# Eighteen pieces of the first five expert tiles multiplied unsplit, conversion's additions on GpSimd too, six products of the identity first

## The chip, the cores and the metric

The program runs on one core of one Trainium2 chip. The metric is the device time of one execution in microseconds; lower is better. [...]

## What is computed

Three layers in float32, one after the other: block-causal attention, an expert layer in which every token goes to one expert, and a dense gated layer.

```python
# attention: q, k, v are (4, 8, 576, 64); position i sees j where i // 64 >= j // 64
scores = np.where(mask, q @ k.T / 8, -1e9)
attn = softmax(scores) @ v
x = attn.transpose(0, 2, 1, 3).reshape(2304, 512)
# experts: expert_emb (8, 512), w1 (8, 512, 1024), w2 (8, 1024, 512), tau 0.1
xn = x / (norm(x) + 1e-6);  en = expert_emb / (norm(expert_emb) + 1e-6)
logits = xn @ en.T / tau
expert_idx = argmax(logits, axis=1);  gate_w = softmax(logits)[expert_idx]
out[mask] = gate_w[mask, None] * (relu(x[mask] @ w1[e]) @ w2[e])   # for each expert e
# dense layer: w_in (512, 2048), w_out (2048, 512)
h = out @ w_in
result = (h / (1 + exp(-h))) @ w_out
```

## The kernel before

**A planner sets every order.** Nothing is issued where it is written. `_Plan` records each operation with the engines that may run it (`either`, `copy`, `tt`, `relu` give two alternatives, `sub` only VectorE), its estimated cost (`_cost`) and what it depends on. `issue` then plays a list schedule: at each step it takes, on the engine that is free first, the ready item with the lowest due time, chooses the engine of items that may go to two, and writes the instructions out in that order. `STAY_NS` is what an item on TensorE is set back by if it needs the array in another shape than the item before (64 rows for scores, 64 columns for the attention's output, the full 128 by 128 for the rest); `CHANGE` is the time that the plan gives such a switch. `_best` builds the program, takes due times from the finished plan backwards (`latest`), builds again, three times in all, and keeps the plan that is shortest by its own estimate. So one changed number can change the order on every engine.

**Precision.** A float32 product is done in one of two ways. Split: both operands are written as a rounded high part and a low rest (`split` for weights: a cast on ScalarE or VectorE and a subtraction on VectorE), and `three` issues three fast products (type fp32r). Unsplit: one product of plain float32, which TensorE runs as two instructions, here without any work on other engines.

**Attention** (`_attention`) handles 16 pairs of heads, staged so that scores of one pair (`s`), transposes of the probabilities of another (`pt`), products with v (`o`) and rows of the output (`e`) of others lie side by side. Softmax takes row maxima on VectorE (`mx`), the exponential on ScalarE (`p`). The norm of the expert embedding is made once, early (`experts`): a square root and a dummy exponential on ScalarE, each of which makes ScalarE load another table of functions.

**Conversion.** `_Convert.piece` rounds the dense layer's weights from raw bits in 32 pieces (16 of `win`, 16 of `wout`), spread over attention and experts. The last step of a piece is an integer addition: on GpSimd for pieces 0 to 11, on VectorE from piece 12 on.

**Experts** (`_layers`). Tokens are sorted into tiles of 128 with one expert each; `_Route` finds the places. For a tile `s`, `xt` transposes the gathered rows (`xg`, two buffers), `first` multiplies with four pieces of w1 (in the order 2, 3, 1, 0), `ht` transposes the hidden rows, `second` multiplies with four pieces of w2. All eight pieces lie in `wraw`, one buffer, refilled for the next tile two pieces at a time if the expert changes. `DIRECT` says how many pieces of each weight of a tile are multiplied unsplit: `(2, 1, 1, 1)`, so pieces 0 and 1 of tile 0 and piece 0 of tiles 1 to 3, for w1 and for w2: ten. Where there are any, `whole` keeps a plain copy of the transposed rows. In PSUM, `xt` and the rest of the tile use the three banks of tag `t`; the banks `a` are for the dense layer's sums. From tile 2 on, chunks of the dense layer (`chunk`: `up` makes `g`, `down` makes `o`) are merged with the tiles.

**The end.** After a chunk's last `down`, `store` copies each of three blocks of the result to SBUF and sends it with an indirect transfer from GpSimd's queue. Just ahead of the transfer, GpSimd copies the column of row numbers (`ix`).

## Time and profile before

| | us |
|---|---|
| median of three runs | 892.42 (892.38 to 893.39) |
| the profiled execution | 892.14 |
| its span, first to last instruction | 890.4 |
| TensorE busy | 856.0 (96%) |
| VectorE busy | 722.6 (81%) |
| ScalarE busy | 554.1 (62%) |
| GpSimd busy | 121.9 (14%) |

The profile is one execution recorded by the hardware; its own time stands 1.7 us above its span. Times in its rows are microseconds from the span's start unless marked ns. PE is TensorE, PEld its weight loads, DVE VectorE, ACT ScalarE, POOL GpSimd, SP SyncE; a q behind the name is the engine's queue. The arrow in `h<-w1s,xt` points from what is read to what is written. The attention fills about the first 210 us; the tiles of the experts run from there to about 610 us, with the dense layer merged in from about 275 us; after that the dense layer is alone. Almost every operation is recorded by one helper line of the planner (L199, or L258 for grouped products), so rows are told apart by the names of the tiles.

### The profile page before, as it was taken

Reading aid. Unit: us, or ns where it says so; the run is one execution under the profiler, and the core shown is the slowest. Engines: PE = TensorE matmul, PEld = TensorE weight load, DVE = VectorE, ACT = ScalarE, POOL = GpSimd, SP = SyncE. Lnnn points to the kernel's source line nnn. Section 1 sums busy time; section 2 is a strip of 40 time slices with the busy share of each in tenths; the row PEclk is TensorE's granted clock in tenths of the full one; section 3 lists DMA queues with packets and bytes.
Section 4 is the critical chain, followed back from the end, with each engine's and each line's share of the span. In section 5 each row is a group of like instructions: output and inputs, shape, how many; then the busy total and the mean of one; then the engine's idle time right before and its main releaser. Section 6 shows DMA issues by size and latency. Waiting matters only on the chain.

```text
span 890.4 us, 13848 instructions
## 1 busy us (share of the span) xinstructions
PE 856.0 (96%) x4986; PEld 713.9 (80%) x4986; DVE 722.6 (81%) x1264; ACT 554.1 (62%) x1128; POOL 121.9 (14%) x162
## 2 busy tenths in 40 slices
PE   5999999999999999999999999999999999999995
PEld 4777677766567888888888888888999999999994
DVE  6989798988999799999888888887677767667672
ACT  7889787976467588888866665665334235334332
POOL 3013131123310000211311111002001001001001
PEclk9999999999999999999999999999999999999998
DMA  6545362473044477530102230342002002000000
GB/s 191 164 122 165 111 180 82 122 256 82 13 159 140 140 272 272 178 94 26 71 24 76 68 119 24 107 132 72 34 1 71 1 1 72 1 0 36 1 1 35
DMA packets 38440, 82.75 MB, mean 93 GB/s; under 512 B 5208, under 2 KB 13400, under 8 KB 38368
## 3 DMA queue, kind: packets, MB, share of 16 engines
q1 hardware_dynamic: 32736, 63.47, 22.2%
q0 software_dynamic: 5632, 18.36, 6.7%
q8 instruction: 40, 0.66, 0.3%
q14 instruction: 32, 0.26, 0.1%
HBM read 123.23 MB, written 13.11 MB: 153 GB/s over the span
## 4 chain that ended last, share of the span: by engine, by line
PE 65%; POOL 0%; POOLq 0%; issue 0%; ACT 0%
PE o L199 22%; PE g L199 22%; PE y L199 9%; PE h L199 9%; PE ht L199 2%; PE xt L199 1%; PE yt L199 1%; POOL out_dram L1559 0%; POOLq L1838 0%; ACT os L199 0%; POOL ix L1558 0%; POOLq L1559 0%
## 5 line engine op out<-in xcount | busy, mean ns | idle before, releaser
L199 PE MATMUL o<-w,g 128*128 128x512 f32 x864 | 234.2, 396 | 0.0
L199 PE MATMUL g<-yt,w 128*128 128x384 f32 x1152 | 230.7, 337 | 0.0
L199 PEld LDWEIGHTS g<-yt,w 128*128 128x128 f32 x1152 | 203.9, 188 | 13.8
L199 PEld LDWEIGHTS o<-w,g 128*128 128x128 f32 x864 | 160.0, 188 | 27.4 <-ACT g L199 0.3
L199 ACT ACTIVATE sg<-g 128x384 f32<-128x384 f32 x96 | 47.4, 494 | 141.9 <-PE g L199 141.8
L199 PE MATMUL y<-w2s,ht 128*128 128x512 f32 x450 | 131.3, 402 | 1.2 <-DVE w2s L199 1.2
L199 PE MATMUL h<-w1s,xt 128*128 128x512 f32 x450 | 110.4, 394 | 3.4 <-DVE xt L199 2.0
L199 PEld LDWEIGHTS h<-w1s,xt 128*128 128x128 f32 x450 | 83.5, 188 | 22.1 <-ACT h L199 2.0
L199 DVE TENSOR_TENSOR w1s<-wraw,w1s 128x1024 fp32r<-128x1024 f32 x75 | 91.2, 1221 | 11.4 <-ACT w1s L199 11.1
L199 DVE TENSOR_TENSOR w2s<-wraw,w2s 128x1024 fp32r<-128x1024 f32 x75 | 91.0, 1224 | 10.0 <-ACT w2s L199 8.7
L199 PEld LDWEIGHTS y<-w2s,ht 128*128 128x128 f32 x450 | 81.2, 188 | 16.3 <-DVE w2s L199 2.7
L199 ACT ACTIVATE p<-s,mx 128x576 f32<-128x576 f32 (+4 forms) x160 | 82.7, 527 | 15.7 <-DVE mx L199 12.9
L199 DVE TENSOR_TENSOR w<-win,w 128x512 fp32r<-128x512 f32 x96 | 66.0, 689 | 24.0 <-ACT w L199 23.4
L199 ACT CAST w2s<-wraw 128x1024 fp32r<-128x1024 f32 x68 | 71.0, 1051 | 14.2 <-PE h L199 7.4
L199 ACT CAST g<-sg 128x384 fp32r<-128x384 f32 x96 | 49.4, 514 | 39.9 <-DVE sg L199 38.3
L258 PE MATMUL s<-ks,qs 64*128 64x288 f32 (+4 forms) x576 | 61.3, 344 | 13.1 <-ACT p L199 7.7
L199 DVE TENSOR_REDUCE mx<-s 128x1 f32<-128x576 f32 (+3 forms) x96 | 64.6, 705 | 10.5 <-PE s L258 9.5
L199 ACT CAST w1s<-wraw 128x1024 fp32r<-128x1024 f32 x53 | 55.6, 1054 | 20.7 <-PE y L199 15.2
L199 DVE TENSOR_TENSOR w<-wout,w 128x512 fp32r<-128x512 f32 x96 | 65.6, 683 | 0.2 <-ACT w L199 0.2
L199 ACT CAST w<-win 128x512 fp32r<-128x512 f32 x75 | 46.6, 625 | 28.7 <-PE o L199 28.6
L258 PEld LDWEIGHTS s<-ks,qs 64*128 64x128 f32 x576 | 46.5, 199 | 20.0 <-ACT p L199 10.5
L199 DVE TENSOR_TENSOR sg<-g,sg 128x384 f32<-128x384 f32 x96 | 53.3, 556 | 10.6 <-ACT sg L199 7.9
(194 smaller groups left out, 1127.5 us busy)
## 6 DMA issues: line engine op xcount, KB each, us to landing
wraw<-in_moe_w_dram SPq DMA_DIRECT2D x76, 1024.0 KB
wbits<-in_moe_w_in_dram SPq DMA_DIRECT2D x16, 512.0 KB
wbits<-in_moe_w_out_dram SPq DMA_DIRECT2D x16, 512.0 KB
k<-in_k_dram SPq DMA_DIRECT2D x16, 288.0 KB
q<-in_q_dram SPq DMA_DIRECT2D x16, 288.0 KB
v<-in_v_dram SPq DMA_DIRECT2D x16, 256.0 KB
x_rows<-xe POOLq DMA_DIRECT2D x16, 256.0 KB, 4.1
wraw<-in_moe_w_dram SPq DMA_DIRECT2D x8, 512.0 KB
```

The costliest lines, as they stand in the source:

```text
L199: alts = {e: (lambda eng, m=m, a=a, k=k: getattr(eng, m)(*a, **k), self._cost(e, m, a, k), self._shares(e, m, a, k) if e != "tensor" else ...
L258: eng.matmul(out, a, b, **kw)
```

## The change

- `DIRECT` becomes `(2, 2, 2, 2, 1)`: eighteen unsplit pieces instead of ten, over five tiles.
- The conversion's addition from piece 12 on may go to VectorE or GpSimd, as the planner finds. So may small additions and products of the routing (`tt`, `ts` of `_Route`).
- Six products of the identity with itself into an unused PSUM tile (`t_warm`) stand first on TensorE. A dummy exponential stands first on ScalarE, and the root of the embedding's norm is made on VectorE by three rounds of a Newton step (`_root`) instead of ScalarE's table.
- `xt` of tiles 2 to 4 uses a bank of tag `a` instead of `t` (`XC = 5`).
- The copies of the row numbers are made when a chunk's first `down` begins; behind each store, GpSimd makes a copy of `ix` to a spare tile.
- The planner: `STAY_NS` 500 and 1500 (two sets of three builds) instead of 2000, `CHANGE` 95 instead of 190, and other costs for some products, reciprocals and subtractions. A term for work that is bound to one engine and still to come (`coming`) has weight 0. Paths under `OM`, `PF`, `CA`, `CB`, `GROOT` are written but not taken.

```diff
-DIRECT = (2, 1, 1, 1)
+DIRECT = (2, 2, 2, 2, 1)
-STAY, STAY_NS, CHANGE = 30, 2000.0, 190.0
+STAY, STAY_NS, CHANGE = 30, 500.0, 95.0
+AD, CA, CB = 1, 0, 0
+GROOT, WARM = 0, 6
+PR = 1
-XC, HC = 0, 0
+XC, HC = 5, 0
...
@@ _cost
-                return 4 * max(n, 32) / 2.4 * part + 3
+                return 4 * max(n, 32) / 2.4 * part + 5
-                return max(n + 32, 2 * free(args[1])) / 2.4 * part
+                if n <= 64:
+                    return 175.0 * part
+                return max(n + 35, 2 * free(args[1]) + 6) / 2.4 * part
...
+def _root(V, z, t, x):
+    zi, xi = z.bitcast(I32), x.bitcast(I32)
+    V.tensor_scalar(zi, xi, 1, None, ALU.logical_shift_right)
+    V.tensor_scalar(zi, zi, float(0x20400000), None, ALU.add)
+    for _ in range(3):
+        V.reciprocal(t, z)
+        V.scalar_tensor_tensor(t, t, 2.0, x, ALU.mult, ALU.mult)
+        V.scalar_tensor_tensor(z, z, 0.5, t, ALU.mult, ALU.add)
...
@@ _Convert.piece
-        (nc.gpsimd if n < 12 else V).tensor_tensor(di, mi, li, ALU.add)
+        if AD and n >= 12:
+            nc.tt(di, mi, li, ALU.add)
+        else:
+            (nc.gpsimd if n < 12 else V).tensor_tensor(di, mi, li, ALU.add)
...
@@ _attention
+    one = cp.tile([P, 1], F32, name="one")
+    nc.vector.memset(one, 0.0)
+    nc.scalar.activation(one, one, AF.Exp)
+    pt = ps_t.tile([P, 512], F32, tag="t", name="t_warm")
+    for _ in range(WARM):
+        nc.tensor.matmul(pt[:, 0:P], ident, ident, start=True, stop=True)
...
-        nc.scalar.activation(en_s[:, 1:2], en_s[:, 0:1], AF.Sqrt)
-        if PRE:
-            nc.scalar.activation(en_s[:, 4:5], en_s[:, 1:2], AF.Exp, scale=0.0)
-        nc.vector.tensor_scalar(en_s[:, 2:3], en_s[:, 1:2], 1e-6, ta, ALU.add, ALU.mult)
+        _root(nc.vector, en_s[:, 1:2], en_s[:, 4:5], en_s[:, 0:1])
+        nc.vector.tensor_scalar(en_s[:, 2:3], en_s[:, 1:2], 0.5, 1e-6, ALU.mult, ALU.add)
+        nc.vector.tensor_tensor(en_s[:, 2:3], en_s[:, 2:3], ta, ALU.mult)
...
@@ _layers, xt
-        bank = "c" if 2 <= s < XC else "t"
+        bank = "a" if 2 <= s < XC else "t"
...
@@ chunk
         def down(*fs):
             if fs[0] == 0:
+                st["ix"] = [wk.tile([P, 1], I32, tag="ix", name=f"ix{a}_{c}", bufs=CH)
+                            for a in range(CH)]
+                for a in range(CH):
+                    nc.gpsimd.tensor_copy(st["ix"][a], st["i"][:, a:a + 1])
...
-                eng.tensor_copy(ix, st["i"][:, a:a + 1])
                 ins = eng.indirect_dma_start(out, IndirectOffsetOnAxis(ap=ix, axis=0), o, None)
...
+                eng.tensor_copy(spare, ix)
```

Since the planner is fed other numbers, the order differs on every engine. Three places follow, of the kernel before and of the changed one.

ScalarE at the program's start, before: `en_s` is the embedding's norm, `p` the probabilities of pair 0, `wcv` a piece of the conversion.

```order
L199 ACT_TABLE_LOAD
L199 CAST ks_142<-k_128 128x576
L199 ACTIVATE qs_143<-q_129 128x576
L199 ACTIVATE esq,en_s<-em 8x512
L199 CAST ks_150<-k_140 128x576
L199 ACT_TABLE_LOAD
L199 ACTIVATE en_s<-en_s 8x1
L199 ACT_TABLE_LOAD
L199 ACTIVATE en_s<-en_s 8x1
L199 ACTIVATE p_152,rs<-s_0_153,mx_4_0_155 128x576
```

ScalarE at the start, now:

```order
L205 ACT_TABLE_LOAD
L205 ACTIVATE one<-one 128x1
L205 CAST ks_144<-k_128 128x576
L205 ACTIVATE qs_145<-q_129 128x576
L205 ACTIVATE esq,en_s<-em 8x512
L205 CAST ks_152<-k_142 128x576
L205 ACTIVATE qs_153<-q_143 128x576
L205 ACTIVATE wcv_166<-wbits_165 128x512
L205 ACTIVATE p_154,rs<-s_0_155,mx_4_0_157 128x576
L205 ACTIVATE p_154,rs<-s_0_156,mx_4_1_158 128x576
```

Two table loads are gone from between the splits and the first probabilities; the split of pair 1's queries and a step of the conversion have come ahead of them.

TensorE at the end of tile 0's first products, before; `h_0` and `h_1` are tiles 0 and 1, `xt` the transposes of a tile's rows, `ht_0` those of tile 0's hidden rows, `ptot` a sum of the routing.

```order
L199 MATMUL h_0_2924<-wraw,x_0_2923 128x512
L199 MATMUL h_0_2925<-wraw,x_0_2923 128x512
L199 MATMUL xt_2928<-ident,xg 128x128 x4
L199 LDWEIGHTS c_ones
L199 MATMUL ptot<-r_oh,c_ones 128x144
L199 MATMUL ht_0_3112<-ident,h_3110 128x128 x4
L199 MATMUL ht_0_3113<-ident,h_3110 128x128 x4
L199 MATMUL h_1_3115<-w1s_2_3117,xt_2929 128x512 x3
L199 MATMUL h_1_3116<-w1s_2_3117,xt_2929 128x512 x3
L199 MATMUL h_1_3115<-w1s_3_3118,xt_2929 128x512 x3
L199 MATMUL h_1_3116<-w1s_3_3118,xt_2929 128x512 x3
```

TensorE at the same place, now:

```order
L205 MATMUL h_0_2933<-wraw,x_0_2932 128x512
L205 MATMUL h_0_2934<-wraw,x_0_2932 128x512
L205 MATMUL xt_2937<-ident,xg 128x128 x4
L205 MATMUL xt_3145<-ident,xg 128x128 x4
L205 MATMUL ht_0_3134<-ident,h_3132 128x128 x4
L205 MATMUL ht_0_3135<-ident,h_3132 128x128 x4
L205 LDWEIGHTS c_ones
L205 MATMUL ptot<-r_oh,c_ones 128x144
L205 MATMUL h_1_3137<-w1s_2_3139,xt_2938 128x512 x3
L205 MATMUL h_1_3138<-w1s_2_3139,xt_2938 128x512 x3
```

The second `xt`, tile 2's, stood directly ahead of tile 2's first products before and now follows tile 1's; tile 3's has moved up likewise, to between tile 1's second and third pieces (ahead of its unsplit ones).

GpSimd at the last three stores, before; `os` is a block of the result, `ix` its row numbers, `yi` where they are copied from.

```order
L1558 COPY ix_5_5392<-yi_5284 128x1
L1559 DMA out_dram<-os_5_5391,ix_5_5392 2304x512
L1558 COPY ix_5_5394<-yi_5284 128x1
L1559 DMA out_dram<-os_5_5393,ix_5_5394 2304x512
L1558 COPY ix_5_5396<-yi_5284 128x1
L1559 DMA out_dram<-os_5_5395,ix_5_5396 2304x512
```

GpSimd at the same place, now (`sp` is the spare copy):

```order
L205 COPY ix_5_5304<-yi_5271 128x1
L205 COPY ix_5_5305<-yi_5271 128x1
L1654 DMA out_dram<-os_5_5381,ix_5_5303 2304x512
L1658 COPY sp_5_5382<-ix_5_5303 128x1
L1654 DMA out_dram<-os_5_5383,ix_5_5304 2304x512
L1658 COPY sp_5_5384<-ix_5_5304 128x1
L1654 DMA out_dram<-os_5_5385,ix_5_5305 2304x512
L1658 COPY sp_5_5386<-ix_5_5305 128x1
```

The copies of the row numbers stand ahead of all three stores, and a spare copy stands behind each.

## Rows read from the trace of the kernel before

**Rows 1.** Windows: start:end, length, busy PE PEld DVE ACT POOL, clock, DMA

```profile
0.00:20.00 20.00, 10.06 (x62) 8.29 (x64) 12.74 (x36) 15.10 (x36) 7.08 (x36) 1.00 0.67 209
20.00:190.00 170.00, 163.23 (x1478) 121.96 (x1478) 152.01 (x343) 141.28 (x428) 34.11 (x33) 1.00 0.47 139
...
211.00:310.00 99.00, 90.94 (x442) 67.12 (x441) 91.43 (x166) 60.82 (x97) 16.36 (x14) 1.00 0.35 112
310.00:400.00 90.00, 90.00 (x450) 77.36 (x449) 85.91 (x122) 77.27 (x120) 11.10 (x10) 1.00 0.62 207
```

**Rows 2.** Timeline of TensorE in the head (start us, length us, what, idle before)

```profile
5.27 1.33 PE L258 MATMUL s<-ks,qs 64*128 64x288 f32 x8 [5.27 <-ACT qs L199]
...
10.92 1.12 PE L258 MATMUL s<-ks,qs 64*128 64x448 f32 x4 [3.63 <-ACT p L199]
...
24.29 0.68 PE L258 MATMUL s<-ks,qs 64*128 64x448 f32 x4 [0.25 <-ACT p L199]
```

**Rows 3.** Timeline of VectorE and ScalarE in the head

```profile
1.42 0.65 DVE L1737 CAST ident<-xg 128x128 fp32r<-128x128 f32 x1 [1.42 <-POOL xg masks.py:199]
...
7.46 0.46 DVE L199 TENSOR_SCALAR qs<-q 128x576 fp32r<-128x576 f32 x1 [1.40 <-DMA q<-in_q_dram]
...
8.51 1.42 DVE L199 TENSOR_REDUCE mx<-s 128x1 f32<-128x576 f32 x2
...
8.66 1.28 ACT L199 ACT_TABLE_LOAD   x1
```

**Rows 4.** Timeline of TensorE at the first unsplit products

```profile
211.45 3.59 PE L199 MATMUL h<-wraw,x 128*128 128x512 f32 x8
214.88 0.60 PE L199 MATMUL xt<-ident,xg 128*128 128x128 f32 x4
```

**Rows 5.** Chain that ended last (start us, length us, what, count)

```profile
304.75 5.46 PE h L199 x24
...
870.53 4.17 PE g L199 x24
```

**Rows 6.** Groups of TensorE between 211 and 310 us (busy, mean ns, idle before)

```profile
L199 PE MATMUL h<-w1s,xt 128*128 128x512 f32 x105 | 27.1, 403 | 3.4 <-DVE xt L199 2.0 <-ACT xt L199 1.4
L199 PE MATMUL y<-w2s,ht 128*128 128x512 f32 x90 | 26.6, 414 | 1.2 <-DVE w2s L199 1.2
L199 PE MATMUL g<-yt,w 128*128 128x384 f32 x60 | 12.1, 337 | 0.0
L199 PE MATMUL y<-wraw,h 128*128 128x512 f32 x20 | 9.8, 596 | 0.0
L199 PE MATMUL h<-wraw,x 128*128 128x512 f32 x20 | 9.4, 592 | 0.0
L199 PE MATMUL o<-w,g 128*128 128x512 f32 x24 | 7.0, 414 | 0.0
L199 PE MATMUL ht<-ident,h 128*128 128x128 f32 x40 | 5.7, 274 | 0.0
L199 PE MATMUL xt<-ident,xg 128*128 128x128 f32 x20 | 3.1, 279 | 2.2 <-DVEq L1623 1.4 <-ACT yr L199 0.8
L199 PE MATMUL yt<-ident,yr 128*128 128x128 f32 x12 | 2.0, 277 | 0.3 <-ACT yr L199 0.3
```

**Rows 7.** Groups of the conversion's additions on VectorE and on GpSimd

```profile
L199 DVE CUSTOM_DVE_ANT_0 wout<-wbits,wcv 128x1024 uint16<-128x1024 uint16 x16 | 11.0, 685 | 0.2
...
L199 POOL TENSOR_TENSOR win<-wcv,wbits 128x512 int32<-128x512 int32 x12 | 15.9, 1325 | 93.0 <-DVE wcv L199 57.7 <-ACT pt L199 16.7 <-DVE ot L199 12.2
```

**Rows 8.** Timeline of GpSimd at its marks of the routing

```profile
184.53 2.78 POOL L199 TENSOR_SCALAR r_rows<-c_nrow,r_prow 128x128 bf16<-128x128 bf16 x4 [9.89 <-DVE r_prow L199]
...
238.06 7.38 POOL L199 TENSOR_SCALAR r_rows<-c_nrow,r_prow 128x128 bf16<-128x128 bf16 x4 [2.82 <-ACT w1s L199]
```

**Rows 9.** Pieces of the second weights split, on VectorE (min/median/max ns)

```profile
L199 DVE TENSOR_TENSOR w2s<-wraw,w2s x75: 1210/1225/1310, 220.9 to 608.6; 128x1024 fp32r<-128x1024 f32 x75
```

**Rows 10.** Timeline of GpSimd at the last stores

```profile
882.16 0.98 POOL L1559 DMA_INDIRECT out_dram<-os,ix  x1 [0.28 <-POOL ix L1558]
```

More of the change, by code (lines that the diff above doesn't have):

```diff
@@ L462, with coming @@
     QUEUE = 1500.0
+    def coming(self, e, t):
+        if not self.fixed:
+            return 0.0
+        n = int(t // BIN)
+        x = self.fixed[e][n:n + BINS]
+        return sum(x) / (BIN * BINS)
     def length(self):
@@ L509, in latest @@
                 put(n)
+        fixed = {e: [0.0] * (int(self.length() // BIN) + BINS + 1) for e in self.ENGINES}
+        for n in live:
+            it = items[n]
+            if not it["dma"] and not it["choice"]:
+                fixed[it["engine"]][int(self.start[n] // BIN)] += it["alts"][it["engine"]][1]
         for _ in live:
@@ L1353, in split @@
         for c in [slice(0, a * b)]:
-            nc.copy(w[:, 0, c], flat[:, c])
+            if CA and a * b == 1024 and CA > int(name.split("_")[1]):
+                nc.scalar.copy(w[:, 0, c], flat[:, c])
+            else:
+                nc.copy(w[:, 0, c], flat[:, c])
             nc.sub(w[:, 1, c], flat[:, c], w[:, 0, c].bitcast(F32))
@@ L1808, in _best @@
 def _best(build):
+    global STAY_NS
     nc, plan = build(None)
-    last = plan
-    for _ in range(ROUNDS):
-        found, last = build(last.latest())
-        if last.length() < plan.length():
-            nc, plan = found, last
+    for STAY_NS in (500.0, 1500.0):
+        last = plan
+        for _ in range(ROUNDS):
+            found, last = build(last.latest())
+            if last.length() < plan.length():
+                nc, plan = found, last
     return nc
```

130 lines of the change are left out of this document (86 added, 44 removed).

## The prediction, made before the result was known

> **What bounds the kernel now.** I read the busy time by stretches first [rows 1]. From 310 us on TensorE is busy without a gap (90.00 of 90.00 between 310 and 400), so there an edit pays only through TensorE's own work. Time that can be won lies in four places: the head (10.06 busy in the first 20 us), the attention (163.23 of 170.00 between 20 and 190, a 6.8 us sum of short waits), the first expert tiles (90.94 of 99.00 between 211 and 310) and the end after the last product. Then I read who waits in the first tiles: TensorE's groups there name VectorE and ScalarE results (`xt`, `w2s`) ahead of the products [rows 6], while VectorE is busy for 91.43 of the same 99.00 us [rows 1]. VectorE's own long pieces are the subtractions of the split, 1.22 us for each piece of weights [rows 9].
>
> More than the visible 8.06 us is free there. Start to start, eight instructions of unsplit products take from 211.45 to 214.88, or 0.429 each [rows 4]; a split product takes 5.46/24 = 0.2275 and a `g` product 4.17/24 = 0.174 where nothing is waited for [rows 5]. With the counts of [rows 6], 219 x 0.2275 + 60 x 0.174 + 40 x 0.429 + 72 transposes x 0.1425 (5.7/40) = 49.8 + 10.4 + 17.2 + 10.3 = 87.7 us of work in 99.0: 11.3 us of slack, part of it hidden inside runs of products that VectorE paces.
>
> **The sum is made against** the profiled execution, 892.14 us (span 890.4, 1.7 around it). The three runs' median is 892.42, 0.03% above, which I neglect.
>
> **Unsplit pieces.** Tiles 1 to 3 get two pieces of each weight unsplit in place of one, tile 4 one in place of none: eight pieces more. A piece is four instructions of 0.429 = 1.72 us unsplit, and six of 0.2275 = 1.37 split, so TensorE gets 8 x 0.35 = **+2.8 us**. VectorE loses eight subtractions, 8 x 1.22 = 9.8 us, and ScalarE or VectorE eight casts. The copies of the transposed rows that unsplit pieces need are only wider. The weights' buffer is not held longer in tiles 1 to 3, because pieces 0 and 1 come in one transfer that already waited for the unsplit product of piece 0.
>
> **What TensorE recovers in the first tiles.** VectorE's 91.4 us there fall by those 9.8 and by about five conversion additions at 0.685 (3.4); the order gives it six more 512-wide passes (four ReLU halves, two casts), at 0.7 each by half of 1.22 and a start, 4.2. That leaves 82, well under the stretch. The other part is order: the transposes `xt` of tile 2 move from directly ahead of its products to behind tile 1's, since tiles 2 to 4 now use an accumulation bank for them. So the 3.4 us before `h` (VectorE's and ScalarE's `xt`) and the 0.8 before `xt` (ScalarE's `yr`) [rows 6] should go. What is late next is TensorE itself. I leave the 1.4 us at the branch (`xt`, released by VectorE's queue) and 2.7 for the routing products and remaining tile starts, and count 11.3 - 4.1 = 7.2 recovered. With the +2.8: **-4.4 us**. Bounds: nothing recovered, +2.8; all but the branch, 9.9 - 2.8 = -7.1.
>
> **Conversion additions.** Sixteen (one of `win`, fifteen of `wout`) move to GpSimd. They free 16 x 0.685 = 11.0 us of VectorE and cost GpSimd 16 x 1.325 [rows 7], in 211 to 400 us, where VectorE stays over 90% busy [rows 1]. GpSimd has the room. The price of two engines at once: four marks `r_rows` took 2.78 us on GpSimd beside the attention's work and 7.38 beside VectorE's splits [rows 8], yet the splits' longest was 1.31 against a median of 1.225 [rows 9]. So GpSimd pays, and VectorE loses at most 0.1 each: 1.6 of 11.0. After 310 TensorE has no gap to fill, so this is worth nothing beyond the line above. Gathers queued behind an addition on GpSimd come up to 2 us later, with most of a tile as cover. The routing's small additions on GpSimd free 2 to 3 us of VectorE and lengthen a chain needed a tile later; nothing.
>
> A rule of the Trainium skill speaks against this part: SBUF — State Buffer, section "Who interferes with whom", says that a VectorE instruction with two SBUF inputs contends with a GpSimd one that reads SBUF, and that whichever comes second is blocked for the whole instruction. By that, VectorE could lose as much as it saves, and the sum would be rival B's 888.9 below; the trace shows the blocking on GpSimd's side only.
>
> **Head: tables.** The square root's table load disappears, and with it the reload of 1.28 us that ended at 9.94, just before the first softmax [rows 3]. What is late next: the order now puts the first row maxima behind pair 1's query subtraction, whose data came only at 7.46 [rows 3]. 7.46, then a cast and a subtraction of 576 columns, about as long as a maximum over 576, which takes 1.42/2 = 0.71, and the maximum itself: 7.46 + 3 x 0.75 = 9.7, against 9.94. **-0.25 us**; bounds -1.3 (one load) and +0.5 (the thirteen tiny root operations cut in).
>
> **Head: six products.** The granted clock reads 1.00 (the 2.4 GHz level) in the first 20 us [rows 1], but the same four score products took 1.12 us at 10.92 and 0.68 at 24.29 [rows 2]; I trust the durations: TensorE ran at about 0.6 of its later rate. Twelve instructions of 128 columns, a quarter of 0.429, doubled at the low rate, are 2.6 us, from the identity's cast at 2.07 [rows 3] to 4.7; the first scores came at 5.27 [rows 2]. So they cost nothing, or 0.4 if slower. What they bring: if all 10.06 busy microseconds ran at the later rate, 10.06 x 0.4 = 4.0 less, but ScalarE is busy for 15.1 of the 20, and after two microseconds of scores TensorE idles for 3.63 [rows 2], in which the rate may be lost again. Between 0.4 lost and 4.0 won I take **-1.0**, nearer to nothing for that gap.
>
> The Trainium skill (TensorE: Matmul & The Clock Gate, section "What's actually happening") says that the throttled clock is the default and that activity lifts it: the durations agree, the granted column does not show it. By the rule alone the whole 4.0 would be in reach and the sum would be rival A's 882.9.
>
> **Attention.** The costs that the planner weighs have changed, so every engine's order differs between 20 and 211 us. The count of product instructions is the same. I take **0**, between -2 and +2: the 6.8 us of waits there [rows 1] could shrink or grow by a third.
>
> **End.** The copies of the row numbers now stand ahead of the last stores, so two stores no longer wait 0.28 for them, of which one stands in [rows 10]; a spare copy takes the old one's place. 2 x 0.28 = **-0.55 us**.
>
> **Sum:** 892.14 - 4.4 - 0.25 - 1.0 + 0 - 0.55 = **885.9 us**.
>
> **Rivals.** (A) *The rate holds from the start.* For it: the slow durations after 10.92; against: the idle 3.63 us. Three more microseconds: 882.9. (B) *Additions on GpSimd block VectorE.* Each addition holds VectorE for 1.325 where it took 0.685: 16 x 0.64 = 10.2 us more, which eats the splits' 9.8; only the order's part of the slack, 4.2 less 2.8, is kept: 892.14 - 1.4 - 1.8 (tables, rate, end) = 888.9. Against it: splits of 1.31 at most. (C) *Half of the slack stays*, because the tile's chain (gather, transposes, cast, subtraction) paces it and not VectorE's load: 3.0 recovered against 2.8 paid, no gain from the rate: 892.14 - 0.2 - 0.8 = 891.1. For it: the waits before `h` name chains, not queues. (D) *Slower: TensorE pays and stands.* TensorE takes its instructions in order, and the `xt` of tiles 2 and 3 now stand ahead of tile 1's unsplit products. Their rows are gathered only once the buffer of two tiles before is free. If a gather is late, everything behind stands, and the slack only moves: +2.8, and about 1 us at each of two tiles, less the end's and tables' 0.8: 896.1. It decides if 9 of the 11.3 us are still idle. Against it: between `xt` of tiles 1 and 3 the order has 22 split products, 22 x 0.2275 = 5 us of work, for one gather to land in. (E) *The moves cancel in the attention:* its waits grow by 4 us: 889.9.
>
> **How the numbers follow.** Forecast 0.48, A 0.15, B 0.09, C 0.14, D 0.08, E 0.06. A measurement of this kernel tells about 0.2%, 1.8 us, from no change, so faster means below 890.4. The forecast, A and B lie below, E mostly; C straddles the bound, within it for two thirds, D above 893.9. Faster 0.80, within 0.12, slower 0.08. The range reaches down to A with the slack's better bound in part, 880.5, and up through C to 891.5; D and the ends beyond are the 2 in 10 left out.
>
> **What would show it.** The stretch from the first split product to 310 us shorter by 4 to 5 us with VectorE under 90% busy; `h` no longer waiting for `xt`; first softmax near 9.7; the four score products after it taking 0.7 rather than 1.1 if the rate held; splits still under 1.35 beside GpSimd's additions; no 0.28 ahead of the last two stores. Wrong would be a first-tiles stretch of the same length with the waits under other names, or attention waits well above 6.8 us.

## The result, and the profile after

The changed kernel took **902.39 us** (median of 4 runs, 899.91 to 904.50) against 892.40 before: 1.0109 of the time before, 95% interval 1.0081 to 1.0137. That is slower by 1.1%; the forecast was 885.9, range 880.5 to 891.5, with a chance of 0.08 on slower. The profiled execution of the changed kernel took 901.68 (span 900.0), that of before 892.14 (890.4).

Starts of the same work in the two traces show where the 9.6 us of the span came from (a pair is one of the attention's 16 pairs of heads; the branch is the program's one `If`, and tile 5 is the first behind it):

| place | before, us | after, us | grown since the place above |
|---|---|---|---|
| first scores of pair 3 | 43.58 | 48.75 | +5.2 |
| last scores of pair 15 | 191.47 | 197.84 | +1.2 |
| first `xt` (tile 0) | 201.04 | 207.35 | -0.1 |
| first `xt` behind the branch (tile 5) | 300.64 | 306.44 | -0.5 |
| end of the last product | 881.2 | 891.2 | +4.3 |
| end of the span | 890.4 | 900.0 | -0.5 |

So the head lost most, the first tiles won 0.5 where 4.4 were forecast, and some 4 us went between the branch and the end, where the prediction expected nothing.

The windows of the kernel after, against [rows 1] (columns: start:end, length, busy PE PEld DVE ACT POOL, clock, DMA share, GB/s):

```profile
0.00:20.00 20.00, 12.11 (x68) 10.08 (x68) 13.45 (x34) 12.90 (x33) 6.72 (x36) 1.00 0.69 212
20.00:190.00 170.00, 163.29 (x1436) 121.77 (x1435) 150.13 (x342) 137.02 (x417) 33.65 (x34) 1.00 0.42 128
211.00:310.00 99.00, 94.73 (x458) 65.31 (x458) 78.52 (x146) 55.56 (x93) 27.77 (x33) 1.00 0.29 97
310.00:400.00 90.00, 88.40 (x430) 73.65 (x429) 84.92 (x111) 69.58 (x107) 24.46 (x16) 1.00 0.62 215
```

From 20 to 190 us TensorE's busy time is what it was, 163.3 of 170, but 42 instructions fewer fit into it: over the whole window TensorE was not idle for longer, it was slower. Inside the window the loss has a place. From the first scores of pair 1 to those of pair 3 lie 23.77 us before and 28.49 after, with the same score products in both; 2.1 of the 4.7 us more are idle time and 2.7 are busy (windows, before and after):

```profile
19.81:43.58 23.77, 23.03 (x196) 17.09 (x195) 22.37 (x49) 18.50 (x56) 2.74 (x2) 1.00 0.50 142
20.26:48.75 28.49, 25.69 (x191) 19.03 (x191) 24.23 (x64) 18.94 (x56) 1.82 (x1) 1.00 0.35 108
```

From there to the first scores of pair 15 the changed kernel is 0.9 us faster, and from those to the last scores 2.1 slower.

VectorE fell from 91.43 to 78.52 in the first tiles, as forecast (82), and TensorE still took about the same stretch. That stretch does not hold quite the same work: behind tile 0's `xt`, the changed order still has twelve instructions that transpose the attention's probabilities, the old one four, and TensorE stood for 1.35 us at them. Between 310 and 400 TensorE has gaps for the first time, 1.6 us, while GpSimd's work has doubled.

TensorE in the head after, against [rows 2] (start us, length us, what, idle before):

```profile
5.34 1.33 PE L264 MATMUL s<-ks,qs 64*128 64x288 f32 x8 [0.29 <-ACT qs L205]
...
12.05 1.11 PE L264 MATMUL s<-ks,qs 64*128 64x448 f32 x4 [4.69 <-ACT p L205]
...
24.73 1.11 PE L264 MATMUL s<-ks,qs 64*128 64x448 f32 x4 [1.11 <-ACT p L205]
...
34.57 0.80 PE L264 MATMUL s<-ks,qs 64*128 64x288 f32 x8
```

The four score products took 0.68 at 24.29 before and 1.11 at 24.73 now; eight of 288 columns are at the later 0.80 only at 34.57. Before, TensorE left the low rate between 22 and 24 us, now between 29 and 34. Eight to ten microseconds more at 0.6 of the rate would be 3 to 4 of the 5.2 us lost by pair 3 (an estimate; the experiments below measure it). The six products ended at 5.06 and changed nothing of it.

The first softmax came later, not earlier ([rows 3]; ScalarE and VectorE):

```profile
8.84 0.68 ACT L205 ACTIVATE qs<-q 128x576 fp32r<-128x576 f32 x1 [1.75 <-DMA q<-in_q_dram]
10.61 0.66 ACT L205 ACTIVATE wcv<-wbits 128x512 f32<-128x512 f32 x1 [1.09 <-DMA wbits<-in_moe_w_in_dram]
11.18 0.73 ACT L205 ACTIVATE p<-s,mx 128x576 f32<-128x576 f32 x1
...
10.23 1.42 DVE L205 TENSOR_REDUCE mx<-s 128x1 f32<-128x576 f32 x2
```

The new order sends for the packed weights `wbits` one transfer earlier, and pair 1's `q` lands at 8.84 in place of 7.46; the maxima wait behind its subtraction, the softmax behind those and behind a conversion step that waits for `wbits`. The table reload is gone and 1.1 us are lost all the same (10.06 to 11.18).

At the last transposes of the probabilities and at tile 0's hidden rows, VectorE and TensorE after:

```profile
209.06 1.06 PE L205 MATMUL pt<-ident,p 128*128 128x128 f32 x8 [1.11 <-DVE xe L205]
...
225.41 1.22 DVE L205 TENSOR_TENSOR w2s<-wraw,w2s 128x1024 fp32r<-128x1024 f32 x1
226.66 0.69 DVE L205 TENSOR_SCALAR h<-h 128x512 f32<-128x512 f32 x1
...
227.50 1.06 PE L205 MATMUL ht<-ident,h 128*128 128x128 f32 x8 [2.44 <-DVE r_oh L205]
...
229.25 1.65 PE L205 MATMUL h<-w1s,xt 128*128 128x512 f32 x6 [0.43 <-DVE xt L205]
```

The forecast's "`xt` no longer waited for" held (between 211 and 310 us, 0.7 in all, of which 0.43 stands here, in place of the 3.4 in [rows 6]), and its warning came true: the wait took another name. Half of the ReLU stands behind a split on VectorE, and TensorE stood for 2.44.

The end came out near the forecast. Two of the last stores now wait 0.16, not 0.28 [rows 10], which is 0.24 in all, and between the last product and the end lie 8.8 us in place of 9.2; the other half of the gain was not followed up:

```profile
891.60 0.99 POOL L1654 DMA_INDIRECT out_dram<-os,ix  x1 [0.16 <-issue]
...
892.94 0.98 POOL L1654 DMA_INDIRECT out_dram<-os,ix  x1 [0.16 <-issue]
```

### The profile page after: what moved, and what is told of

Same layout as the page of the kernel before. It is cut to its first block, busy times and chain, and to the rows that moved or that the text cites. A ratio compares the mean times of both kernels' runs of the same rounds, so it can differ in the third digit from the quotient of the medians.

```text
span 900.0 us, 13867 instructions
## 1 busy us (share of the span) xinstructions
PE 866.8 (96%) x4982; PEld 716.6 (80%) x4982; DVE 716.4 (80%) x1241; ACT 548.8 (61%) x1116; POOL 162.0 (18%) x211
## 4 chain that ended last, share of the span: by engine, by line
PE 55%; DVE 1%; issue 0%; ACT 0%; POOL 0%; POOLq 0%; DVEq 0%; ACTq 0%
PE o L205 20%; PE g L205 19%; PE y L205 7%; PE h L205 6%; PE ht L205 1%; PE yt L205 1%; PE xt L205 1%; DVE w1s L205 0%; DVE w L205 0%; POOL out_dram L1654 0%; DVE wcv L205 0%; DVE ht L205 0%; ACT wcv L205 0%; ACT ys L205 0%; ACT os L205 0%
## 5 line engine op out<-in xcount | busy, mean ns | idle before, releaser
L205 PE MATMUL y<-w2s,ht 128*128 128x512 f32 x426 | 127.0, 406 | 0.0
L205 PE MATMUL h<-w1s,xt 128*128 128x512 f32 x426 | 106.9, 397 | 1.9 <-DVE w1s L205 1.3
L205 DVE TENSOR_TENSOR w1s<-wraw,w1s 128x1024 fp32r<-128x1024 f32 x71 | 89.9, 1271 | 13.3 <-ACT w1s L205 12.7
L205 PEld LDWEIGHTS h<-w1s,xt 128*128 128x128 f32 x426 | 78.5, 188 | 21.2 <-DVE w1s L205 3.5
L205 DVE TENSOR_TENSOR w<-win,w 128x512 fp32r<-128x512 f32 x96 | 70.8, 739 | 25.3 <-ACT w L205 24.8
L205 PEld LDWEIGHTS y<-w2s,ht 128*128 128x128 f32 x426 | 76.8, 188 | 15.9 <-issue 3.1
L205 DVE TENSOR_REDUCE mx<-s 128x1 f32<-128x576 f32 (+2 forms) x96 | 65.0, 706 | 15.3 <-PE s L264 11.5
L205 ACT CAST w1s<-wraw 128x1024 fp32r<-128x1024 f32 x57 | 59.8, 1052 | 24.5 <-PE y L205 10.7
L205 ACT CAST g<-sg 128x384 fp32r<-128x384 f32 x95 | 48.9, 514 | 41.8 <-DVE sg L205 40.1
L205 ACT CAST w2s<-wraw 128x1024 fp32r<-128x1024 f32 x61 | 63.9, 1051 | 10.9 <-PE h L205 10.3
L205 PE MATMUL pt<-ident,p 128*128 128x128 f32 (+1 forms) x400 | 63.0, 294 | 4.4 <-DVE pt L205 1.1
L205 ACT CAST w<-win 128x512 fp32r<-128x512 f32 x78 | 48.5, 623 | 29.6 <-PE o L205 29.3
L1654 POOL DMA_INDIRECT out_dram<-os,ix x18 | 20.1, 1115 | 255.8 <-ACT os L205 251.4
```

What stands on the lines that cost most here:

```text
L205: alts = {e: (lambda eng, m=m, a=a, k=k: getattr(eng, m)(*a, **k), self._cost(e, m, a, k), self._shares(e, m, a, k) if e != "tensor" else ...
L1654: ins = eng.indirect_dma_start(out, IndirectOffsetOnAxis(ap=ix, axis=0), o, None)
```

## The experiments

Since every edit makes the planner order all engines anew, an edit alone cannot be told from its new order. So most of these kernels hold the order: the place and engine of each step are written down as the planner had left them and replayed, and only the steps named are moved, added or given to another engine. "Held after" and "held before" name the order held. In e8, e11, e12 and e17 only the first 820 steps (to about 152 us) are held and the planner orders the rest; in e4 and e15 it orders everything. "The level" is the granted clock of TensorE, which has two values here, 1.00 (2.4 GHz) and 0.50 (1.2 GHz); a window that spans both reads a figure between. Times are medians; ratios are against the kernel before, run on the same chip in the same session. Starts are those of the profiled execution:

| | pair 3 | last scores | `xt` 0 | `xt` 5 | last product ends | time | ratio, 95% interval |
|---|---|---|---|---|---|---|---|
| before | 43.6 | 191.5 | 201.0 | 300.6 | 881.2 | 892.4 | |
| after | 48.8 | 197.8 | 207.4 | 306.4 | 891.2 | 902.4 | 1.0081 to 1.0137 |
| e1 | 48.9 | 197.2 | 206.2 | 308.3 | 893.2 | 903.8 | 1.0103 to 1.0136 |
| e2 | 48.9 | 197.1 | 206.2 | 308.2 | 893.1 | 901.3 | 1.0050 to 1.0102 |
| e3 | 48.5 | 197.7 | 206.7 | 306.7 | 888.4 | 898.8 | 1.0039 to 1.0075 |
| e4 | 48.6 | 199.1 | 210.9 | 305.5 | 889.7 | 900.0 | 1.0033 to 1.0078 |
| e5 | 48.7 | 197.3 | 206.3 | 306.4 | 891.2 | 901.6 | 1.0081 to 1.0128 |
| e6 | 41.0 | 188.3 | 197.8 | 299.6 | 880.3 | 890.7 | 0.9966 to 0.9991 |
| e7 | 43.0 | 190.2 | 199.7 | 301.4 | 884.9 | 895.3 | 1.0020 to 1.0040 |
| e8 | 43.5 | 191.6 | 202.7 | 298.1 | 880.1 | 890.6 | 0.9971 to 0.9990 |
| e9 | 49.6 | 198.2 | 207.2 | 307.3 | 892.2 | 903.4 | 1.0098 to 1.0131 |
| e10 | 48.6 | 196.6 | 205.6 | 307.7 | 892.6 | 902.4 | 1.0079 to 1.0113 |
| e11 | 43.3 | 195.1 | 208.6 | 307.7 | 888.3 | 899.3 | 1.0041 to 1.0076 |
| e12 | 42.0 | 189.4 | 200.2 | 295.7 | 877.7 | 890.0 | 0.9955 to 0.9981 |
| e13 | 45.3 | 193.6 | 202.6 | 302.7 | 887.7 | 898.0 | 1.0032 to 1.0073 |
| e14 | 43.2 | 191.1 | 200.6 | 300.2 | 880.9 | 891.9 | 0.9985 to 1.0004 |
| e15 | 41.1 | 197.6 | 216.3 | 311.0 | 891.4 | 903.4 | 1.0110 to 1.0152 |
| e16 | 45.1 | 196.1 | 205.1 | 305.5 | 887.3 | 897.1 | 1.0034 to 1.0068 |
| e17 | 41.6 | 189.7 | 202.5 | 298.0 | 879.9 | 890.3 | 0.9966 to 0.9985 |

### The head's order (e1) and the six products (e2), held after

```diff
 SP
-wbits_0  k_2  ta  q_2
+k_2  ta  q_2  wbits_0
 VectorE
-qs_1  mx_0  mx_0
+mx_0  mx_0  qs_1
 ScalarE
-wcv_0  p_0  p_0
+p_0  p_0  wcv_0
```

> The changed kernel with the place of every instruction written down as it stood, and five of them moved in the head: the transfer of the first packed weights goes behind pair 2's query, the first two row maxima ahead of pair 1's query subtraction on VectorE, the first two softmax passes ahead of the weights' conversion on ScalarE (its two VectorE steps behind the row maxima). Theory 'late head' (the head's order kept TensorE idle for 4.69 us after its first scores, and its products at the low rate to about 31 us in place of 23): first softmax near 10.1 in place of 11.2, the idle gap near 3.7, pair 3 starts at about 44 in place of 48.75, whole time 902.4 - 4 to 5 = 897.5 to 898.5. Theory 'order of the attention' (each pair's waits are set by the planner's costs, wherever the head begins): pair 3 at 47.5 or later, whole time 901 to 903.

```diff
-    for _ in range(WARM):
-        nc.tensor.matmul(pt[:, 0:P], ident, ident, start=True, stop=True)
```

> The changed kernel, the place of every other instruction as it stood, without the six products of the identity. If the products bring the rate nothing, as the score products of 1.11 us at 24.7 say: the same within 1 us, 901.5 to 903.5, and the first scores still at 5.3. If they bring the 1.0 us of the prediction: 903.4. If they themselves delay the later rate (they end at 5.06, and TensorE then idles): a microsecond or more faster, below 901.

In e1 the second scores came at 9.78 in place of 12.05, and pair 3 still at 48.9: second scores more than two microseconds earlier were worth nothing, so "late head" falls. e2 is within its runs (897.6 to 903.5) the same as after: the six products bring nothing. Both profiles show what after's had only in its durations, the lower level; here e2 (windows, as above):

```profile
20.00:25.00 5.00, 3.79 (x28) 3.17 (x29) 3.64 (x12) 3.22 (x8) 0.00 (x0) 1.00 0.54 164
25.00:30.00 5.00, 5.00 (x42) 4.62 (x40) 3.99 (x14) 2.50 (x7) 0.00 (x0) 0.60 0.40 125
30.00:35.00 5.00, 4.06 (x24) 3.14 (x22) 4.14 (x11) 4.09 (x16) 0.00 (x0) 0.50 0.00 0
35.00:40.00 5.00, 5.00 (x35) 2.61 (x34) 4.43 (x10) 2.28 (x6) 1.82 (x1) 0.87 0.20 59
```

The level had risen by 24.3 (four score products in 0.68) and fell to 0.50, 1.2 GHz, until 36 us.

### The gaps filled (e5, e9, e13: held after; e6: held before)

```diff
+    fill = ps_o.tile([P, 512], F32, tag="t", name="t_fill")
...
+    nc.tensor.matmul(fill[:, 0:P], ident, ident, start=True, stop=True)
```

> The changed kernel, the place of every instruction as it stood, with twelve more products of the identity on TensorE, into a bank that nothing uses yet: ten in the idle gap behind the first scores (4.69 us, ten at the low rate take 4.9) and two in the gap before pair 1's second scores. Theory 'low rate' (the changed kernel loses in the head because its TensorE stands still often enough to stay at the 1.2 GHz level until 33 us, where the kernel before leaves it at 22 to 24): the granted clock reads 1.00 from 15 us on, the four score products at 24.7 take 0.68 in place of 1.11, pair 3 starts at 44 to 45 in place of 48.75, whole time 902.4 - 4 to 5 = 897.5 to 898.5. Theory 'waits' (other engines pace the first pairs, and a faster TensorE waits longer): pair 3 still at 48 or later, whole time 901 to 904.

> The kernel before, the place of every instruction as it stood, with fourteen products of the identity on TensorE: six ahead of the first scores, as in the change, and eight in the idle gap of 3.63 us behind them. Theory 'low rate': the level rises before 11 us instead of at 22 to 24, the four score products at 10.92 take 0.68 in place of 1.12, and of some 9 us of TensorE's work between 11 and 22 us 0.4 is saved: 892.4 - 2 to 4 = 888.5 to 890.5. Theory 'waits': below 1 us, 891.5 to 893.

> As the changed kernel with twelve more products, but twenty-one: seventeen in the gap behind the first scores (4.4 us, of which twenty instructions at the high rate had filled 2.5) and four ahead of pair 1's second scores. Theory 'low rate': the level, once up, stays up; the products behind 12.7 us keep the high rate (pt groups of four 0.66 in place of 1.12), pair 3 at 44 to 46 in place of 48.7, whole time 3 to 4 us below that of the run with twelve, 897.5 to 898.5. Theory 'waits': pair 3 at 48 or later, 901 to 903.

> As the changed kernel with twenty-one more products of the identity, but thirty: seventeen behind the first scores, four, one and two ahead of pair 0's transposes (where TensorE stood for 1.41, 0.18, 0.65 and 0.21 while the level fell from 16.8 us on) and six ahead of pair 1's second scores. Theory 'low rate': the level stays up past 17 us, pair 3 at 43 to 46 in place of 48.7 to 49.6, whole time 3 to 5 us below the run with twenty-one: 898.5 to 900.5. If other engines pace the first pairs: pair 3 at 47 or later, 902 to 904.

By their times alone, e5 and e9 come out as "waits" has it; their rows show that the level had not held, so they do not decide. In e5 it rose before 6 us, the products were through at 8.9, TensorE stood for 1.94, and from 12.7 on the rate was low again. In e9 it held to 16.8, fell there behind waits of 1.41, 0.18 and 0.65, and stayed down to 36 us, although TensorE was busy without a gap from 22 to 31: pair 3 at 49.6. In e13 the gaps behind 15 us were filled too, and the level held (TensorE; two instructions to a product; then the window from pair 1 to pair 3):

```profile
7.27 6.08 PE L713 MATMUL t_fill<-ident 128*128 128x128 f32 x34
13.28 0.67 PE L264 MATMUL s<-ks,qs 64*128 64x448 f32 x4
...
23.33 0.68 PE L264 MATMUL s<-ks,qs 64*128 64x448 f32 x4
...
45.33 0.80 PE L264 MATMUL s<-ks,qs 64*128 64x288 f32 x8
```

```profile
19.91:45.33 25.42, 22.91 (x203) 16.40 (x203) 24.00 (x63) 19.18 (x57) 1.82 (x1) 1.00 0.39 119
```

Pair 3 came at 45.3 although the second scores came 1.2 us later than in after, and the time fell by 4.4 to 898.0, or by 5.4 against e9, which has nine products fewer. The order on every engine is the same, and nothing is faster but TensorE: 3.4 of the 5.2 us lost by pair 3 are the low level's. The rest is still there, as waits: from pair 1 to pair 3 TensorE is idle for 2.5 us in e13, 0.7 in before. In the order of before, e6 raised the level at 11 us, and pair 3 came 2.6 us earlier; of this and the 0.6 won later, 1.6 is left at the end (890.7, between the two forecasts). The level now fell in two places where it had held in before. At 215 us this cost 0.4, since later waits took up the rest; at 250 us, behind waits of 0.39 and 0.53, it cost 1.6 (e6, and the same products of before):

```profile
10.85 0.82 PE L258 MATMUL s<-ks,qs 64*128 64x448 f32 x4
...
215.62 4.58 PE L199 MATMUL h<-w1s,xt 128*128 128x512 f32 x12 [1.78 <-DVE xt L199]
...
249.87 5.96 PE L199 MATMUL h<-w1s,xt 128*128 128x512 f32 x18
```

```profile
218.62 3.01 PE L199 MATMUL h<-w1s,xt 128*128 128x512 f32 x12 [1.79 <-DVE xt L199]
...
252.56 4.35 PE L199 MATMUL h<-w1s,xt 128*128 128x512 f32 x18
```

### The additions (e3: held after, e7: held before)

```diff
 pieces 12 and 17 to 31
-nc.gpsimd.tensor_tensor(di, mi, li, ALU.add)
+nc.vector.tensor_tensor(di, mi, li, ALU.add)
```

> The changed kernel, the place of every instruction as it stood, but the sixteen conversion additions that had gone to GpSimd run on VectorE at the same places. Theory 'blocking' (VectorE's splits of 1.27 in place of 1.22 us and its other two-input work are slowed beside GpSimd's additions; some 8 us of VectorE's time between 211 and 420 us): splits back at 1.22, whole time 2 to 3 us less, 899.5 to 900.5, won between 211 and 420 us. Theory 'VectorE is full' (the additions are work that VectorE has no room for): 16 x 0.69 = 11 us more on VectorE, whole time 2 to 5 us more, 904 to 907. The rows of the additions are not in an order chosen for this, so part of a loss would be the order's.

e7 has the opposite edit in the order of before.

> The kernel before, the place of every instruction as it stood, but the same sixteen conversion additions that the change moves run on GpSimd. Theory 'blocking' (GpSimd's additions slow VectorE's two-input instructions beside them by more than the 0.69 each that they free): splits at 1.25 or more in place of 1.22, whole time 1 to 4 us more, 893.5 to 896.5, lost between 310 and 420 us, where VectorE is busy all the time. The prediction's step (VectorE loses at most 0.1 each, TensorE has no gap there): within 1 us, 891.5 to 893.5.

Moving them back won 3.6 us, moving them alone cost 3.0; in both, the stretch behind the branch shows as much (from `xt` 5 to the last product 584.8 after, 581.7 in e3; 580.5 before, 583.5 in e7), and TensorE's idle time is 1.7 and 2.0 of it. VectorE's splits tell how (min/median/max ns, first and last start; after, e3, e7):

```profile
L205 DVE TENSOR_TENSOR w1s<-wraw,w1s x38: 1209/1218/2344, 207.3 to 429.4; 128x1024 fp32r<-128x1024 f32 x38
```

```profile
L205 DVE TENSOR_TENSOR w1s<-wraw,w1s x38: 1211/1218/1306, 206.8 to 426.6; 128x1024 fp32r<-128x1024 f32 x38
```

```profile
L199 DVE TENSOR_TENSOR w1s<-wraw,w1s x41: 1207/1217/2824, 214.3 to 428.8; 128x1024 fp32r<-128x1024 f32 x41
```

The median did not move; single ones doubled. One place of after, GpSimd and VectorE:

```profile
344.75 1.32 POOL L205 TENSOR_TENSOR wout<-wcv,wbits 128x512 int32<-128x512 int32 x1 [2.66 <-DVE wcv L205]
...
345.00 1.62 DVE L205 TENSOR_TENSOR w<-win,w 128x512 fp32r<-128x512 f32 x1
```

VectorE's subtraction of 0.685 begins 0.25 us behind the addition and ends 0.55 behind the addition's end, so by these times it stood until GpSimd was almost done. Where the addition comes second it stands itself (2.17 in place of 1.32), and in e7 TensorE then waited for the delayed split (GpSimd, VectorE, TensorE):

```profile
341.81 2.17 POOL L199 TENSOR_TENSOR wout<-wcv,wbits 128x512 int32<-128x512 int32 x1 [5.27 <-DVE wcv L199]
...
342.72 3.47 DVE L199 TENSOR_TENSOR w2s<-wraw,w2s 128x1024 fp32r<-128x1024 f32 x2
...
345.12 0.96 PE L199 MATMUL y<-w2s,ht 128*128 128x512 f32 x3 [1.13 <-DVE w2s L199]
```

This is rival B's mechanism. The Trainium skill (SBUF — State Buffer, "Who interferes with whom") says that a VectorE instruction with two SBUF inputs contends with a GpSimd one that reads SBUF, that the port they share is an exclusive lock, and that the order of issue decides who waits; the trace agrees, in both directions. Beside the fifteen additions behind 200 us, eleven VectorE instructions of after are longer than the median of their kind, by 10.2 us in all, and twelve of e7, by 12.3. That is about the 11.0 us which the additions had freed: VectorE's busy time is 724.5 us in e7 and 722.6 in before, 716.4 in after and 715.4 in e3. The kernel loses because the delays come at places that nobody chose, some of them just ahead of TensorE. The routing's small operations that moved to GpSimd as well were not tried alone.

### The unsplit pieces (e8), the reordering (e11), the planner's numbers (e4, e15)

```diff
-DIRECT = (2, 1, 1, 1)
+DIRECT = (2, 2, 2, 2, 1)
-XC, HC = 0, 0
+XC, HC = 5, 0
-        bank = "c" if 2 <= s < XC else "t"
+        bank = "a" if 2 <= s < XC else "t"
```

> The kernel before with only the unsplit pieces (2, 2, 2, 2, 1 in place of 2, 1, 1, 1) and the bank for the transposes of tiles 2 to 4; its own planner, with the attention's first 820 steps (to about 152 us) held in the order in which they stood, the rest ordered anew. The prediction's step: first tiles 4.4 us shorter, 888.0, between 885.3 and 895.2 by its bounds. Rival C (the tile's chain paces, not VectorE's load): 891 to 892.5. Rival D (TensorE pays 2.8 us and stands as long as before): 895 or more.

From `xt` 0 to `xt` 5, with the same tiles in it, the stretch fell from 99.6 to 95.5: 4.1 us, as the prediction had it (4.4). The kernel won 1.7; by its time alone it lies nearer to rival C than to the prediction's step. Ahead of the stretch 1.6 us were lost, at the low level (0.50 to 0.82 between 190 and 200), and 1.5 behind it, whose cause I did not find; TensorE's idle time explains 0.45 of it.

The order behind 152 us is also another one in e8. e11 is the control for that: no edit of the program at all, only that order is new.

> The kernel before with nothing changed but the order: the first 820 steps held, the rest (from about 152 us) ordered anew by its own planner, whose other start leads it to another order of 323 rows' difference on TensorE. It tells how much time an order alone is worth: if orders are as good as one another, 891.5 to 893.5; if an order is worth as much as the parts measured so far (1.7 to 3 us), outside of that.

From `xt` 0 to `xt` 5 it took 99.1, so a new order by itself need not shorten that stretch. It cost 6.5 us (899.3), all of it ahead of `xt` 0: a wait of 2.27 for the last pair's softmax and the low level behind it (TensorE, then the windows):

```profile
191.41 1.11 PE L258 MATMUL s<-ks,qs 64*128 64x448 f32 x4 [2.27 <-ACT p L199]
```

```profile
190.00:200.00 10.00, 8.59 (x60) 7.66 (x60) 7.06 (x18) 5.23 (x19) 2.86 (x4) 0.55 0.89 315
200.00:210.00 10.00, 9.33 (x60) 5.78 (x59) 6.35 (x13) 6.63 (x14) 0.53 (x1) 0.77 0.40 154
```

The planner's numbers were exchanged in both programs: in e4 the changed program is ordered with the old ones, in e15 the old program with the new ones.

```diff
-STAY, STAY_NS, CHANGE = 30, 2000.0, 190.0
+STAY, STAY_NS, CHANGE = 30, 500.0, 95.0
...
-                return max(n + 32, 2 * free(args[1])) / 2.4 * part
+                return max(n + 35, 2 * free(args[1]) + 6) / 2.4 * part
...
+    for STAY_NS in (500.0, 1500.0):
```

> The changed kernel with the planner's numbers of the kernel before: its costs of an instruction, the price of a change of operand form (190 and 2000 in place of 95 and 500) and its one search in place of two; all other parts of the change as they are. Theory 'order' (the loss comes from the planner's new costs): the attention's end near 193 in place of 198.3, whole time below 892.4 + 2, down to the 885.9 that was forecast. Theory 'parts' (the unsplit pieces, GpSimd's additions and the head lose by themselves): 900 or more, the last score still at 197 or later.

> The kernel before with nothing changed but the planner's numbers and search, which are those of the changed kernel: the same work, ordered anew on every engine. Theory 'order' (the loss is that of a new order, whatever the parts; the re-ordered kernel of before, 899.3, speaks for it): 897 to 904, pair 3 at 47 or later or the last score at 195 or later. Theory 'parts': 891 to 894.

The old program with the new numbers took 903.4, **11 us more with no operation added or taken away**. It lost otherwise than after: the level rose at 22 us and pair 3 came early (41.1), but then TensorE waited at the transposes of the probabilities (`pt`) for VectorE's and ScalarE's copies of earlier ones and of the attention's output (`ot`) (groups from 50 to 200 us; before, after, e15; busy, mean ns, idle before):

```profile
L199 PE MATMUL pt<-ident,p 128*128 128x128 f32 (+1 forms) x312 | 45.8, 279 | 1.2 <-DVE pt L199 0.8 <-ACT p L199 0.2 <-ACT ot L199 0.2
```

```profile
L205 PE MATMUL pt<-ident,p 128*128 128x128 f32 x312 | 45.6, 280 | 1.1 <-ACT ot L205 0.7 <-DVE pt L205 0.2
```

```profile
L199 PE MATMUL pt<-ident,p 128*128 128x128 f32 (+1 forms) x302 | 45.0, 279 | 7.1 <-DVE pt L199 2.1 <-DVE ot L199 1.2 <-ACT ot L199 1.1
```

e4 shows that the old numbers do not bring the old time back either: another order again, 900.0, last scores at 199.1, as "parts" has it; e15 came out as "order" has it. Neither theory holds for both; a new order was dear whichever numbers made it.

### The ReLU first (e10, held after) and the head's part alone (e14, held before)

```diff
 VectorE, tile 0
-w2s cast  r_idx  w2s split  h
+h  w2s cast  r_idx  w2s split
```

> The changed kernel, the place of every instruction as it stood, but the half of tile 0's ReLU that VectorE computes stands ahead of the cast and the split of the second matrix's third piece, not behind them. In the changed kernel its 0.69 us began at 226.66, 2.4 us after the last product it reads, and TensorE's transposes of tile 0 stood for 2.44. Theory 'queue' (the first tiles' gain was taken back by this wait, and by the granted clock of 0.57 to 0.75 that followed it in other runs): the wait below 0.7, the stretch from the first xt to the branch 1.5 to 4 us shorter, whole time 898.5 to 901. Theory 'load' (what the split then lacks is waited for a moment later): within 1 us of 902.4.

"Load" holds. The wait of 2.44 and 0.43 became three that sum to 2.70 (TensorE):

```profile
224.00 1.07 PE L205 MATMUL ht<-ident,h 128*128 128x128 f32 x8 [0.57 <-DVE h L205]
225.87 0.41 PE L205 MATMUL ptot<-r_oh,c_ones 128*128 128x144 bf16 x1 [0.81 <-DVE r_oh L205]
...
227.61 2.93 PE L205 MATMUL h<-w1s,xt 128*128 128x512 f32 x6 [1.32 <-DVE xt L205]
```

What followed these waits sets the stretch's length. After, e3 and e2 have the same order here, and the same wait of 2.44. The granted clock of 225 to 235 us reads 1.00 in after, 0.83 in e3 and 0.66 in e2, and `xt` 0 to `xt` 5 took 99.1, 100.0 and 102.1 (102.1 in e10 too, also at 0.66):

```profile
225.00:235.00 10.00, 7.13 (x37) 5.74 (x37) 9.88 (x25) 5.17 (x11) 3.75 (x6) 1.00 0.33 89
```

```profile
225.00:235.00 10.00, 8.09 (x35) 6.90 (x36) 9.18 (x22) 4.69 (x9) 2.94 (x6) 0.83 0.29 77
```

```profile
225.00:235.00 10.00, 8.20 (x27) 6.31 (x28) 8.71 (x23) 4.04 (x8) 2.35 (x6) 0.66 0.23 68
```

So executions of this order differ by up to 3 us at this place alone, with the same waits. That may be most of the 4.6 us between the changed kernel's shortest and longest run; only one of those was profiled, so it is not shown.

```diff
-        nc.scalar.activation(en_s[:, 1:2], en_s[:, 0:1], AF.Sqrt)
+        _root(nc.vector, en_s[:, 1:2], en_s[:, 4:5], en_s[:, 0:1])
+    nc.scalar.activation(one, one, AF.Exp)
+    for _ in range(6):
+        nc.tensor.matmul(fill[:, 0:P], ident, ident, start=True, stop=True)
```

> The kernel before, the place of every instruction as it stood, with the head's part of the change alone: the square root by eleven small VectorE operations at the place of ScalarE's, the exponential's table loaded by a first use at the start, six products of the identity first. If the head's part itself costs what the changed kernel lost: first softmax late, TensorE at the low rate to 33 us, pair 3 at 47 or later, 896 to 898. The prediction's steps (tables -0.25, products -1.0): 891. If the tables alone help (p no longer behind the reload, at 9.4 in place of 10.06) and the products do nothing: 891.5 to 892.5, pair 3 at 42.5 to 43.6.

The third case: first softmax at 9.61 in place of 10.06, 0.5 us at the end for tables and products together, not to be told from nothing.

### Put together (e12, e17) and repaired (e16)

e12 is the kernel before with e8's pieces and order, e6's fourteen products, and the early copies of the row numbers; e17 fills more gaps of its head. e16 is e13 and e3 in one.

```diff
-DIRECT = (2, 1, 1, 1)
+DIRECT = (2, 2, 2, 2, 1)
...
+    nc.tensor.matmul(fill[:, 0:P], ident, ident, start=True, stop=True)
...
+                    nc.gpsimd.tensor_copy(st["ix"][a], st["i"][:, a:a + 1])
```

> The kernel before with three things: the unsplit pieces in the order measured before (890.6), the fourteen products of the identity in the head (890.7 alone), and the row numbers copied ahead of the last stores (0.47 at the end of the changed kernel). If they add: 892.3 - 1.7 - 1.6 - 0.5 = 888.5. If what the head gains is given back by a clock that falls after a gap between 186 and 250 us: 890 to 890.5.

> The combined kernel (889.99: unsplit pieces, fourteen products, row numbers copied early) with twenty-eight products in place of fourteen: eleven behind the first scores and eleven in the gaps up to pair 1's second scores. In the combined kernel the granted clock read 0.63 and 0.69 between 15 and 25 us; if the gaps let it fall, it now stays up and pair 3 starts at 41 or before in place of 42.0: 888 to 889.5. If the products stand in the way more than they hold: 890 to 891.5.

> The changed kernel, the place of every instruction as it stood, with two repairs at once: thirty products of the identity that fill TensorE's gaps in the head (898.0 alone, 4.4 below the changed kernel) and the sixteen additions on VectorE (898.8 alone, 3.6 below). If the two losses are separate and make up most of the whole: 902.4 - 4.4 - 3.6 = 894.4, between 893 and 896. If they are one loss seen twice: 897 to 899.

e12 is the best of all, **889.99, 0.9968 of before (0.9955 to 0.9981)**; its parts add in part only (2.8 us of 3.8). e17 did not better it: what its head won (pair 3 at 41.6) went at the low level behind 188 us (0.50 to 0.81 between 185 and 200). e16's whole time, 897.1, is the one forecast for a single loss seen twice. Its rows say otherwise: the additions' 3.2 us are there (581.8 from `xt` 5 to the last product, 585.0 in e13), but 2.6 went ahead of `xt` 0, where the clock read 0.50 between 180 and 185. The two losses are separate, and their repairs do not sum in the whole time, since the level fell in another place.

## Why the prediction was wrong

- **Attention, 0 +/- 2: the step that failed first.** It counted the instructions, found them the same, and let the waits vary by a third of 6.8 us. Over 20 to 190 us the waits did stay (6.7), but the last scores came 6.4 us late. What was missed is that an order also sets when TensorE works at which level: with the same order and the level held, e13 had 3.4 us back by pair 3 and 4.4 at the end. Missed too is that waits can gather in one place (2.1 us more between pairs 1 and 3), and that an order may be worth far more than a third of its waits (e11 +6.5, e15 +11, with no other edit). Rival E named the place but expected longer waits, priced them at 4, and gave it 0.06.
- **What stays open of the 10 us.** The parts sum to 0.3: additions +3.0, unsplit -1.7, head -0.5, end -0.5, the first and third in the order of before. That the rest is the order's is argued from this sum and from e11 and e15, not shown: e16, with the head's gaps filled and the additions back, still took 4.6 us more than before, 4.1 of them lost by `xt` 0, and these were not taken apart.
- **Six products, -1.0 (0.4 to -4.0): 0.** The row was read rightly (0.6 of the rate up to 22 us) and so was the objection, the idle 3.63 behind the first scores. e6 and e13 show that products do raise and hold the level when they fill the gaps too. The Trainium skill (TensorE: Matmul & The Clock Gate, "What's actually happening") says that the throttled clock is the default and activity lifts it; e5 and e6 agree (the level rose there before 6 us and at 11 us). But once lifted it did not stay up through the next waits, 1.94 in e5 and 1.41 in e9, and rival A's rate from the start did not come.
- **Conversion additions, 0 with at most 0.1 each: +3.0 to +3.6. The second step that failed.** The step went by splits of at most 1.31 beside GpSimd's marks [rows 8, 9]. Those marks read one tensor, the additions two; splits beside the additions took up to 2.82, and not one above 1.31 where no addition overlapped it. Rival B's mechanism is shown. Its price, 10.2 us more for VectorE than before, is not: some additions come second and wait themselves, and the delays about use up what was freed. The step "after 310 TensorE has no gap to fill, so this is worth nothing" had no place for a delay that opens such gaps.
- **Unsplit pieces and first tiles, -4.4: right for the edit (-4.1 in e8), -0.5 in the changed kernel.** VectorE's load fell as reckoned. The changed order's stretch is 3.6 us longer than e8's. About 2.5 of that (an estimate) is attention work which the order left behind `xt` 0: eight transposes more at some 0.15 each, and 1.35 us of waits; that is no loss of the tiles. At tile 0 the order dealt VectorE the casts and splits all at once, 2.87 us of waits at one place, which only move when one of them is moved (e10). And a stretch's gain is not the kernel's: e8 kept 1.7 of it.
- **Tables, -0.25: 0.45 earlier at the first softmax in the old order (e14), 1.1 later in the new one**, where an earlier transfer delayed what the forecast took to land at 7.46. By e1 even that cost nothing in the end.
- **End, -0.55: -0.47.** Near in size; but the two waits fell by 0.12 each and not by 0.28, so half of it came by another way.

Open stays what makes the level rise at 22 us in one order and stay up, and only at 32 to 37 in others; in e4 TensorE worked from 24.1 to about 32 without a gap and at the low level. Fillers at other gaps (188, 215, 227, 250 us) were not tried.

## What to carry to other kernels

Where a scheduler orders the program, measure an edit in a held order, and a mere reordering beside it, before the edit is credited or blamed; here orders were worth up to 11 us and edits 0.5 to 4. Sum TensorE's work at the level that the durations show, and reckon that a wait on it can cost more than its length, by the products behind it (1.6 us in e6, behind waits of 0.39 and 0.53). Two-input GpSimd work beside a VectorE that is hardly ever idle was not free here: look for single instructions of double length, the median hides them.
